# Group 0 of an attention + MoE kernel: triples of rows, transposes by half pairs between the scores, w1(0) between the value loads

## The chip, the cores and the metric

The kernel runs on one core of a Trainium2 chip. The metric is device time in microseconds (us) of one execution; the median of several runs counts. Profiles show single executions: TensorE (PE, with its weight loads as PEld), VectorE (DVE), ScalarE (ACT), GpSimd (POOL) and SyncE (SP), which only issues DMAs here.

## What is computed

Attention with two kinds of heads, and a mixture of experts on its result:

```
q, k, v: [4 batches, 8 heads, 768 tokens, 64] fp32
heads 0, 2, 6 ("retrieval"):     causal attention over all keys
heads 1, 3, 4, 5, 7 ("streaming"): causal, only the first 4 keys (sinks)
                                   and a window of 64 keys
a   = softmax(q k^T / 8, masked); attn = a v
x   = attn as [3072 tokens, 512]
out = sum over 4 experts e of  p_e * (relu(x @ w1_e) @ w2_e)
      w1_e: [512, 1024], w2_e: [1024, 512], p = domain_probs / their sum
```

## The kernel before

Attention is done in eight groups, a batch's half of 384 rows each. The order of the instructions on every engine is written out by hand: `attention(b, c)` is a generator that yields after every piece of work, and a plan runs it either alone or between pieces of MoE work. Group 0 runs alone, as nothing else has its inputs yet. Behind it comes the first MoE stage, `plain_steps`: three row tiles times expert 0, 1, 2, ..., each with w1(e) (matmul L1095) and w2(e) (L1116); group 1's attention is put between these matmuls. Up to some 55 us this stage needs weights that are still being loaded. Later MoE stages use sums of weights and other lines (L1229, L1258, L1409), and the change does not touch them.

**x in blocks.** x stands transposed in `xT`, four blocks of 128 rows. Block 0 holds heads 0 and 4, block 1 heads 1 and 5, block 2 heads 2 and 6, block 3 heads 3 and 7. The first MoE matmuls take four tiles of hidden columns together, with the blocks in the order 0, 2, 1 for each, and block 3 of all four at the end.

**Group 0, step by step.**

- *Rows of q and k.* `q32` and `k32` lie in `hA`, which the MoE uses only later. One DMA for each head loads its 384 rows as three blocks of 128 tokens (partition p, block j: token 128 j + p); a packet is one row of 64 fp32, 256 bytes. SyncE's queue issues k of all heads and q of heads 4 to 7, ScalarE's queue q of heads 0 to 3.
- *Transposes* (`transposes(hp)` for head pair hp): three fp32 `nc.tensor.transpose` for q and three for k (L576), each for 128 tokens and two heads, into one PSUM bank `ps`. VectorE or ScalarE then evict the bank as f16 to `qT` (L594), `kR` (retrieval keys, L602) or `kS` (streaming keys, L618), and the four sink keys beside them (L626).
- *Scores* (L693 for q and k, L705 for the mask, which is added by a matmul with the identity). ScalarE takes Exp (L711) into `es`.
- *Values* of a retrieval head (L756): 65 columns, of which the last is the sum. VectorE divides (L781 to L785), into `x_one` or `x_pair`, and `x_transposes` (L805, L809) bring them into `xT`. Values of a streaming head (L828) come out transposed, with the sums in the other half of the partitions: ScalarE takes Ln (L846) and Exp of minus that (L856, or L861 for two heads at once), and VectorE multiplies into `xT` (L851, "scaling").
- *Warm-up matmuls* (`warm_up`, L448): products of zeros, 8 at the start, 5 before scores 0, 8 before scores 2, and some of 256 columns before values of heads 3, 4, 5, 6, 7.
- *Masks*: `bC` (causal) and `bS` (streaming, three tiles of 160 columns) are made on GpSimd before its loads (L457 to L509).

**GpSimd's loads.** GpSimd's queue casts fp32 to f16 while it loads. Its order is: v of head 0, the masks, v of heads 2, 1, 3, 4, 6, 5, 7, w1(0) as two DMAs (the two halves of the partitions), w2(0), clears for group 1, w1(1). After that, one-element copies `landed(...)` (L521, "seen") make GpSimd wait until a load is there before it issues more: after w1(0) come k and q of heads 0 to 3 of group 1, after w2(0) comes w2(1), after these q the other heads, v and w1(2), and so on up to w2(2) and w1(3).

**Group 1** already loads "triples": `load_triples` gives partition p the tokens 3p, 3p + 1, 3p + 2, in a row in memory, for four heads at a time. Its transposes are f16 matmuls of half width (64 columns of lhsT, one head each, rhs the identity, L579), so that a bank holds the tokens in the order j, p; VectorE puts them in order while it evicts (L594, L602, L618 with rearranged views).

Of the kernel before, what the change touches and what calls it, by code (L numbers as in the profile page):

```python
# [11 lines left out]
FP32 = mybir.dt.float32  # L12
# [7 lines left out]
def kernel(  # L20
# [33 lines left out]
    nc = tc.nc  # L54
# [259 lines left out]

    def sink_row(h):

        t = v_tiles(0, 0, h)
        nc.vector.tensor_copy(
            out=t[0:NS, :, own_v(h)],
            in_=v_s32[:, h : h + 1, :].to_broadcast([NS, TC, D]),  # L320
        )
# [9 lines left out]

    def load_w1(e, f0, f1):
        x = moe_w1[e].rearrange("(u c d) f -> u d c f", u=2, c=DMP)
        for u in range(2):
            gp.dma_start(
                out=w1sb[half(u), e * DMP : (e + 1) * DMP, f0:f1],
                in_=x[u, :, :, f0:f1],
            )
# [61 lines left out]
    def rows32(n):  # L400
        x = hA[:, n * 6 * H * D : (n + 1) * 6 * H * D].bitcast(FP32)
        return x.rearrange("p (j h d) -> p j h d", j=3, h=H)

    q32, k32 = rows32(0), rows32(1)
    v_s32 = early[0:NS, 0:1024].bitcast(FP32).rearrange("p (h d) -> p h d", h=H)
    for h in range(H):
        if h == 2:
            nc.sync.dma_start(
                out=v_s32, in_=v[0, :, 0:NS, :].rearrange("h r d -> r h d")
            )  # L410
        nc.sync.dma_start(out=k32[:, :, h, :], in_=rows_of(k, 0, h, 0))
        if h == HP:

            nc.scalar.add_instruction(
                mybir.InstLoadActFuncSet(
                    name=nc.get_next_instruction_name(),
                    engine=ENG.Activation,
                    act_func_set_id=[x.name for x in SETS].index(
                        "natural_log_exp_and_others"
                    ),  # L420
                )
            )
        eng = nc.scalar if h < HP else nc.sync
        eng.dma_start(out=q32[:, :, h, :], in_=rows_of(q, 0, h, 0))
    nc.sync.dma_start(
# [6 lines left out]
    )  # L432
    nc.vector.memset(warm.bitcast(FP32), 0.0)
    nc.vector.memset(eps, 1e-9)
    nc.vector.memset(ones, ONES)
# [3 lines left out]
    zero(nc.vector, kR[0][:, 0, :, :, :])  # L439
    zero(nc.vector, kS[:, 0, :, :, :])  # L440
    nc.vector.tensor_copy(out=ident16, in_=ident32)
# [12 lines left out]

    def mask_c(x, keep, drop):

        gp.memset(x, keep)  # L457
        for i in range(2):
            gp.affine_select(
                out=x[:, i * P : (i + 1) * P], in_=x[:, i * P : (i + 1) * P],  # L460
                compare_op=ALU.is_ge, fill=drop, base=0, pattern=[[1, P]],
                channel_multiplier=-1,
            )

    def mask_s(x, n, keep, drop):

        gp.memset(x, keep)
        gp.affine_select(
            out=x, in_=x, compare_op=ALU.is_ge, fill=drop,
            base=R0, pattern=[[0, n], [1, TQ]], channel_multiplier=-1,  # L470
        )
        gp.affine_select(
            out=x, in_=x, compare_op=ALU.is_ge, fill=drop,
            base=NW - 1 - R0, pattern=[[0, n], [-1, TQ]], channel_multiplier=1,
        )
        gp.memset(x[0:R0, :, :], drop)
        gp.memset(x[0:NS, :, 0:TK], keep)
        gp.affine_select(
            out=x[0:NS, 0, 0:TK], in_=x[0:NS, 0, 0:TK], compare_op=ALU.is_ge,
            fill=drop, base=-NW, pattern=[[1, TK]], channel_multiplier=-1,  # L480
        )
# [24 lines left out]

    mask_c(bC, 0.0, -60000.0)
    mask_s(bS[:, 0:2, :], 2, 0.0, -60000.0)
    gp.tensor_copy(out=bS[:, 2, :], in_=bS[:, 1, :])  # L509
    load_v(0, 0, [2, 1, 3, 4, 6, 5, 7])  # L510
    load_w1(0, 0, F)
    load_w2(0)
# [45 lines left out]
    def attention(b, c):  # L558
# [8 lines left out]
        def transposed(x, hp):  # L567

            if first or hp > 1:
                ps = bank()  # L570
            else:
                ps = pV.tile([P, 512], FP32, name="pV", bufs=2)
            for j in range(3):
                o = ps[:, j * P : (j + 1) * P]
                if first:
                    nc.tensor.transpose(o, x[:, j, 2 * hp : 2 * hp + 2, :], ident32)  # L576
                    continue
                for u in range(2):
                    nc.tensor.matmul(  # L579
                        out=o[u * D : (u + 1) * D, :],  # L580
                        lhsT=x[:, 2 * hp + u, j, :],
                        rhs=ident16,
                        start=True,
                        stop=True,
                    )
            return ps

        def transposes(hp):
            both_at_once = [] if first else [transposed(x, hp) for x in (qt16, k16)]
            for x, is_k in ((q32 if first else qt16, 0), (k32 if first else k16, 1)):  # L590
                ps = transposed(x, hp) if first else both_at_once[is_k]
                if not is_k:
                    op = nc.scalar.copy if first and hp < 2 else nc.vector.tensor_copy
                    op(out=rows_in_order(qTs[b, c][:, hp, :]), in_=cols(ps))  # L594
                    if first:
                        yield t_ns
                    continue
                for u in range(2):
                    h = 2 * hp + u
                    r = slice(u * D, (u + 1) * D)  # L600
                    if RETR[h]:
                        nc.vector.tensor_copy(  # L602
                            out=rows_in_order(
                                kR[i][r, c, RH.index(h), :, :].rearrange(
                                    "r t x -> r (t x)"
                                )
                            ),
                            in_=cols(ps[r, :]),
                        )
                        continue  # L610
                    n = SH.index(h)
                    x_in, x_out = ps[r, 0:CH], kS[r, c, :, n, R0:P]
                    if first:
                        x_in = x_in.rearrange("r (t x) -> r t x", x=TK)
                    else:
                        x_in = x_in.rearrange("r (j t p) -> r j t p", j=3, t=TC)
                        x_out = x_out.rearrange("r t (p j) -> r j t p", j=3)
                    nc.vector.tensor_copy(out=x_out, in_=x_in)  # L618
# [6 lines left out]
                    src = src.rearrange("r (o x) -> r o x", o=1)  # L625
                    op(out=sinks, in_=src.to_broadcast([D, TC, NS]))  # L626
                yield 2 * t_ns if first else 3 * t_ns

        def rows_in_order(x):

            return x if first else x.rearrange("r (p j) -> r j p", j=3)

        def cols(x):
            x = x[:, 0:CH]
            return x if first else x.rearrange("r (j p) -> r j p", j=3)


        def score_tiles(h):
# [39 lines left out]
            ]  # L678

        es_of = {}  # L680
        pv_of = {}
        rc_of = {}
        scale_of = {}
        def scores(h):
            hp = h // 2
            es_of[h] = []
            for cols, parts, masks in score_tiles(h):
                ps = bank()
                if first and not es_of[h]:
                    warm_up(ps, {0: 5, 2: 8}.get(h, 0), P)  # L690
                ns = 0
# [119 lines left out]
        def values(h):  # L811
# [29 lines left out]
            r, o = half(u), half(1 - u)  # L841
            pair = first and h in (3, 4)
            if not pair or u == 0:
                rc_of[0] = att.tile([P, CH], FP32, name="rc", bufs=2)
            rc = rc_of[0]
            nc.scalar.activation(  # L846
# [11 lines left out]
            elif u == 0:  # L858
                scale_of[0] = scale
            else:  # L860
                nc.scalar.activation(out=rc, in_=rc, func=AF.Exp, scale=-1.0)  # L861
                later(scale_of[0], g)
                later(scale, g)
# [16 lines left out]
        if first:  # L880
            yield from transposes(0)
            yield from scores(0)
            sink_row(1)
            sink_row(3)
            yield from transposes(1)
            yield from scores(2)
            sink_row(4)
            sink_row(5)
            sink_row(7)
            yield from both(scores(1), values(0))  # L890
            yield from transposes(2)
            yield from both(scores(3), values(2))
            x_transposes(0)
            yield from scores(4)
            yield from transposes(3)
            yield from values(1)
            yield from both(scores(5), values(3))
            yield from both(scores(6), values(4))
            yield from both(scores(7), values(6))
            yield from values(5)  # L900
            at_once = behind.pop()
            v_steps = values(7)
            yield next(v_steps)
            x_transposes(6)
            at_once[1]()
            yield from v_steps
            tick(LAG)
# [760 lines left out]
```

## Time and profile before

| | |
|---|---|
| median of 3 runs | 376.3 us (376.27 to 376.65) |
| the profiled execution | 377.82 us |
| its span in the trace | 376.10 us |
| clock granted to TensorE | 1.00 |
| first MoE matmul starts | 21.50 us |
| TensorE busy | 367.1 us, 98% of the span |
| VectorE, ScalarE, GpSimd busy | 281.6, 227.3, 112.9 us |
| HBM, mean over the span | 136 GB/s |

Times in the profile count from the start of the span. A line such as "33.75 0.36 PE L579 MATMUL ... x6 [0.16 <-DMA q]" says: from 33.75 us, for 0.36 us, six matmuls of line 579 on TensorE, which before them stood idle for 0.16 until a DMA into q had landed. Matmuls are pipelined and their ends modelled, so the distance between starts tells more than the durations. In the table by stretches, each engine has its busy time and its instructions, then the clock granted to TensorE, the share of the DMA engines and GB/s. In the list of the chain each piece has its start, its length and what it was.

### The profile page before, as it was taken

Reading aid. Unit: us, or ns where it says so; the run is one execution under the profiler, and the core shown is the slowest. Engines: PE = TensorE matmul, PEld = TensorE weight load, DVE = VectorE, ACT = ScalarE, POOL = GpSimd, SP = SyncE. Lnnn points to the kernel's source line nnn. Section 1 sums busy time; section 2 is a strip of 40 time slices with the busy share of each in tenths; the row PEclk is TensorE's granted clock in tenths of the full one; section 3 lists DMA queues with packets and bytes.
Section 4 is the critical chain, followed back from the end, with each engine's and each line's share of the span. In section 5 each row is a group of like instructions: output and inputs, shape, how many; then the busy total and the mean of one; then the engine's idle time right before and its main releaser. Section 6 shows DMA issues by size and latency. Waiting matters only on the chain.

```text
span 376.1 us, 10310 instructions
## 1 busy us (share of the span) xinstructions
PE 367.1 (98%) x4221; PEld 312.4 (83%) x4221; DVE 281.6 (75%) x589; ACT 227.3 (60%) x475; POOL 112.9 (30%) x155
## 2 busy tenths in 40 slices
PE   8889999999999999999999999999999999999996
PEld 4755556568998999999989899988899998998996
DVE  7774768697788569868657858957767968989882
ACT  3863478557785785765676955774678362450630
POOL 8923664793058038115601650320000000000000
DMA  8999999999599579988904991971220200300101
GB/s 157 159 208 207 179 186 194 180 201 121 90 104 164 97 83 133 153 111 63 205 12 61 169 156 16 131 129 12 68 72 2 92 24 2 114 2 0 58 3 58
DMA packets 123748, 39.25 MB, mean 104 GB/s; under 512 B 113728, under 2 KB 116356, under 8 KB 123700
## 3 DMA queue, kind: packets, MB, share of 16 engines
q0 software_dynamic: 85824, 19.01, 58.6%
q1 hardware_dynamic: 36276, 19.18, 23.3%
q8 instruction: 33, 0.54, 0.7%
q10 hardware_dynamic: 1600, 0.39, 0.5%
q14 instruction: 15, 0.12, 0.1%
HBM read 44.89 MB, written 6.34 MB: 136 GB/s over the span
## 4 chain that ended last, share of the span: by engine, by line
PE 78%; DMA 12%; DVE 5%; POOL 3%; issue 1%; ACT 0%; DVEq 0%; POOLq 0%
PE pO L1409 29%; PE pA L1229 20%; PE pO L1258 9%; PE pO L1116 5%; DMA q<-in_q_dram 5%; PE pA L693 4%; DMA w2sb<-in_moe_w_dram 4%; PE pA L1095 3%; DMA w1sb<-in_moe_w_dram 2%; PE pV L1258 2%; PE pA L1258 2%; DVE xs L1180 2%; PE pV L828 2%; PE pV L756 2%; DMA xT<-x_pair 1%
## 5 line engine op out<-in xcount | busy, mean ns | idle before, releaser
L1409 PEld LDWEIGHTS <-hA 128*128 128x128 f16 x1104 | 104.9, 98 | 11.9
L1229 PE MATMUL pA<-xs,w1sb 128*128 128x256 f16 x768 | 97.1, 272 | 0.0
L1229 PEld LDWEIGHTS <-w1sb 128*128 128x128 f16 x768 | 71.7, 98 | 7.3
L1409 PE MATMUL pO<-w2sb,hA 128*128 128x256 f16 x640 | 76.8, 272 | 0.0
L711 ACT ACTIVATE es<-pA 128x384 f16<-128x384 f32 (+2 forms) x122 | 59.2, 512 | 26.4 <-PE pA L693 23.2
L1238 ACT ACTIVATE hA<-pA 128x512 f16<-128x512 f32 x96 | 57.2, 597 | 29.6 <-PE pA L1229 27.3
L306 POOL DMA_DIRECT2D vS<-in_v_dram x30 | 29.6, 986 | 113.7 <-PE pV L828 110.5
L1409 PE MATMUL pO<-tsb,hA 128*128 128x256 f16 x464 | 56.8, 272 | 0.0
L1180 DVE TENSOR_TENSOR xs<-xT,pB 128x1024 f16<-128x1024 f16 (+1 forms) x49 | 47.0, 977 | 3.7 <-DMA xT<-x_pair 3.7
L1014 DVE TENSOR_TENSOR hA<-hA 128x1024 f16<-128x1024 f16 x60 | 39.4, 684 | 0.6 <-PE pO L1409 0.3
L1108 ACT ACTIVATE hA<-pA 128x384 f16<-128x384 f32 (+1 forms) x64 | 22.2, 385 | 20.3 <-PE pA L1095 20.2
L1258 PEld LDWEIGHTS <-w1sb 128*128 128x128 f16 x512 | 31.3, 98 | 2.1 <-DVE xs L1014 0.8
L1095 PE MATMUL pA<-xT,w1sb 128*128 128x384 f16 (+1 forms) x256 | 30.4, 272 | 2.0 <-DMA w1sb<-in_moe_w_dram 1.9
L1116 PE MATMUL pO<-w2sb,hA 128*128 128x512 f16 x128 | 30.6, 379 | 0.1
L1095 PEld LDWEIGHTS <-w1sb 128*128 128x128 f16 x256 | 19.5, 98 | 11.0 <-issue 2.6
L1429 ACT COPY s<-pO 128x256 f32<-128x256 f32 x31 | 11.5, 372 | 27.3 <-PE pO L1409 21.8
L851 DVE TENSOR_TENSOR xT<-pV,rc 64x384 f16<-64x384 f32 x37 | 20.5, 554 | 9.3 <-ACT rc L856 6.8
L722 DVE TENSOR_TENSOR es<-es,mS 128x384 f16<-128x384 f16 (+1 forms) x40 | 13.8, 344 | 18.0 <-ACT es L711 17.9
L846 ACT ACTIVATE rc<-pV,eps 64x384 f32<-64x384 f32 x37 | 21.3, 575 | 7.0 <-PE pV L828 6.4
L1275 DVE CUSTOM_DVE_ANT_0 hA<-pO,s 128x512 f16<-128x512 f32 x26 | 17.7, 688 | 9.9 <-PE pO L1258 8.5
L1268 ACT COPY s<-pO 128x512 f32<-128x512 f32 x39 | 22.7, 588 | 3.2 <-PE pO L1258 3.0
L693 PE MATMUL pA<-qT,kR 128*128 128x128 f16 (+2 forms) x141 | 23.1, 261 | 0.4 <-DVE kR L602 0.4
(170 smaller groups left out, 527.6 us busy)
## 6 DMA issues: line engine op xcount, KB each, us to landing
pB<-p_rows SPq DMA_DIRECT2D x10, 512.0 KB
out_dram<-o SPq DMA_DIRECT2D x19, 256.0 KB
w1sb<-in_moe_w_dram POOLq DMA_DIRECT2D x8, 512.0 KB, 9.2
w2sb<-in_moe_w_dram POOLq DMA_DIRECT2D x4, 1024.0 KB, 13.3
vS<-in_v_dram POOLq DMA_DIRECT2D x30, 112.0 KB, 4.8
k_rows<-in_k_dram POOLq DMA_DIRECT2D x18, 128.0 KB, 5.1
q<-in_q_dram POOLq DMA_DIRECT2D x18, 128.0 KB, 6.4
vR<-in_v_dram POOLq DMA_DIRECT2D x24, 48.0 KB, 5.5
```

The source lines that it names most:

```text
L306: gp.dma_start(out=t[:, :, own_v(h)], in_=windows_of(v, b, h, c))
L693: nc.tensor.matmul(out=ps[:, o : o + nq], lhsT=key_tile(b, c, h, t), rhs=qTs[b, c][:, hp, q0 : q0 + nq], start=(n == 0 or not first), stop ...
L711: nc.scalar.activation(out=es[:, 0:cols], in_=ps[:, 0:cols], func=AF.Exp, scale=SC)
L1014: nc.vector.tensor_tensor(out=out, in0=a, in1=b, op=ALU.subtract)
L1095: nc.tensor.matmul(out=pss[ft][:, 0:cols_n], lhsT=w1_tile(e, ct, ft), rhs=x[:, ct, :], start=(n == 0), stop=(n == DMP - 1),)
L1116: nc.tensor.matmul(out=ps_o, lhsT=hs[:, ft, j * P : (j + 1) * P], rhs=w2sb[:, e * FTP + ft, :], start=(ft == 0), stop=(ft == FTP - 1),)
L1180: nc.vector.tensor_tensor(out=o, in0=xin, in1=pb.to_broadcast([P, DMP, n, P]), op=ALU.mult)
L1229: nc.tensor.matmul(out=ps[:, f * PC : (f + 1) * PC], lhsT=w1_tile(e, ct, f0 + f), rhs=xs[:, ct, :], start=(ct == 0), stop=(ct == DMP - 1),)
L1238: nc.scalar.activation(out=blocks[:, b0 : b0 + 2, k0 : k0 + 2, :].rearrange("p t f x -> p f t x"), in_=ps.rearrange("p (f t x) -> p f t x" ...
L1258: nc.tensor.matmul(out=ps[:, f * P : (f + 1) * P], lhsT=w_tile(e, w[:, ct, :], f), rhs=a[:, ct, :], start=(first and f == 0 and ct == 0), ...
L1268: nc.scalar.copy(out=kept[n], in_=ps)
L1409: nc.tensor.matmul(out=ps, lhsT=a[:, k, :], rhs=b(k), start=(first and k == 0), stop=(k == KT - 1), skip_group_check=not first,)
```

## The change

1. *Triples of rows for group 0.* q and k of heads 2 to 7 are loaded two heads at a time, partition p with the tokens 3p, 3p + 1, 3p + 2 (768 bytes in a row): six DMAs instead of twelve. Heads 0 and 1 stay as they were.
2. *Transposes by half pairs.* For these heads a block of q or k is transposed by six fp32 matmuls, each of one head's 64 columns with the fp32 identity, instead of three `transpose`. They write the bank with a stride of three columns, in the natural order of the tokens. Group 1's f16 halves do the same, and all evictions read the bank straight. In group 0 these blocks use the two banks of pool `pO`.
3. *Order.* Before, both halves of a pair (q and k) were transposed together. Now the blocks stand one by one between the scores: q of heads 2, 3; scores 0; k of 2, 3; scores 1; q of 4, 5; scores 2; k of 4, 5; scores 3 and values 0; q of 6, 7; scores 4; k of 6, 7; scores 5 and values 2; values 1; scores 6 and values 4; values 3; scores 7 and values 6; values 5; x transposes of head 6; values 7. Three warm-up matmuls stand before scores 0, none before scores 2.
4. *Sinks.* Five copies of sink rows of v become three larger ones, earlier. The copies of sink keys of heads 1 and 3 are put off to a set place.
5. *Masks.* One memset on VectorE clears both masks; the streaming mask is cut out of one tile of 160 columns and then copied, the last copy on VectorE. `kS` is cleared in four pieces.
6. *Loads.* v of 2, 1, 3; first half of w1(0); v of 4, 6; second half; v of 5, 7; w2(0).
7. *Exp for two heads at once* for heads 1 with 4 and 3 with 5, instead of 3 with 4.

The diff, cut:

```diff
-    for h in range(H):
+    for h in range(0, H, 2):
...
-        nc.sync.dma_start(out=k32[:, :, h, :], in_=rows_of(k, 0, h, 0))
+        pair_of_triples(nc.sync, k, k32, h)
...
+    def pair_of_triples(eng, x, dst, h):
+        if h == 0:
+            for u in range(2):
+                eng.dma_start(out=dst[0][:, :, u, :], in_=rows_of(x, 0, u, 0))
+            return
+        eng.dma_start(
+            out=dst[1][:, h - 2 : h, :, :].rearrange("p h j d -> p h (j d)"),
+            in_=x[0, h : h + 2, 0:CH, :].rearrange("h (p j) d -> p h (j d)", j=3),
+        )
...
+    nc.vector.memset(early[:, 1536:2272].bitcast(FP32), 0.0)
...
-    zero(nc.vector, kS[:, 0, :, :, :])
+    for t in range(TC):
+        zero(nc.vector, kS[:, 0, t : t + 1, :, :])
...
-    mask_s(bS[:, 0:2, :], 2, 0.0, -60000.0)
-    gp.tensor_copy(out=bS[:, 2, :], in_=bS[:, 1, :])
-    load_v(0, 0, [2, 1, 3, 4, 6, 5, 7])
-    load_w1(0, 0, F)
+    mask_s(bS, 0.0, -60000.0)
+    nc.vector.tensor_copy(out=bS[:, 2, :], in_=bS[:, 1, :])
+    load_v(0, 0, [2, 1, 3])
+    load_w1(0, 0, F, 0)
+    load_v(0, 0, [4, 6])
+    load_w1(0, 0, F, 1)
+    load_v(0, 0, [5, 7])
     load_w2(0)
...
-            if first or hp > 1:
+            if first and hp:
+                ps = pO.tile([P, 512], FP32, name="pO", bufs=2)
+            elif first or hp > 1:
                 ps = bank()
...
+            natural = ps[:, 0:CH].rearrange("r (x j) -> r j x", j=3)
             for j in range(3):
-                o = ps[:, j * P : (j + 1) * P]
-                if first:
-                    nc.tensor.transpose(o, x[:, j, 2 * hp : 2 * hp + 2, :], ident32)
+                o = natural[:, j, :]
+                if first and hp == 0:
+                    nc.tensor.transpose(
+                        ps[:, j * P : (j + 1) * P], x[0][:, j, :, :], ident32
+                    )
                     continue
                 for u in range(2):
                     nc.tensor.matmul(
                         out=o[u * D : (u + 1) * D, :],
-                        lhsT=x[:, 2 * hp + u, j, :],
-                        rhs=ident16,
+                        lhsT=x[1][:, 2 * hp - 2 + u, j, :] if first else x[:, 2 * hp + u, j, :],
+                        rhs=ident32 if first else ident16,
...
-                    warm_up(ps, {0: 5, 2: 8}.get(h, 0), P)
+                    warm_up(ps, {0: 3}.get(h, 0), P)
...
-            pair = first and h in (3, 4)
+            pair = first and {1: 1, 4: 1, 3: 3, 5: 3}.get(h)
...
             yield from transposes(0)
+            yield from transposes(1, 0)
+            put_off.pop(0)()
+            sink_row(1, 2)
             yield from scores(0)
-            sink_row(1)
-            sink_row(3)
-            yield from transposes(1)
+            yield from transposes(1, 1)
+            sink_row(4, 2)
+            sink_row(7)
+            yield from scores(1)
+            put_off.pop(0)()
+            yield from transposes(2, 0)
             yield from scores(2)
...
+            yield from values(1)
+            yield from both(scores(6), values(4))
             x_transposes(0)
-            yield from scores(4)
-            yield from transposes(3)
-            yield from values(1)
-            yield from both(scores(5), values(3))
-            yield from both(scores(6), values(4))
+            yield from values(3)
             yield from both(scores(7), values(6))
             yield from values(5)
-            at_once = behind.pop()
-            v_steps = values(7)
-            yield next(v_steps)
             x_transposes(6)
-            at_once[1]()
-            yield from v_steps
+            yield from values(7)
```

## The prediction, made before the changed kernel ran

> **What bounds the kernel now.** I read the page first (busy shares and the chain that ended last), then TensorE's waits, then the timeline of the first 55 us, because the diff touches only group 0 and what is loaded beside it.
>
> ```profile
> span 376.1 us, 10310 instructions
> PE 367.1 (98%) x4221; PEld 312.4 (83%) x4221; DVE 281.6 (75%) x589; ACT 227.3 (60%) x475; POOL 112.9 (30%) x155
> PE 78%; DMA 12%; DVE 5%; POOL 3%; issue 1%; ACT 0%; DVEq 0%; POOLq 0%
> ```
>
> TensorE is busy 98% of the span, so what is not TensorE work is small. The chain holds 12% of transfers, and its list in time order shows where:
>
> ```profile
> 12.53 8.84 DMA w1sb<-in_moe_w_dram
> 22.40 11.30 DMA q<-in_q_dram
> ...
> 41.02 13.57 DMA w2sb<-in_moe_w_dram
> 54.63 1.02 PE pO L1116 x4
> ```
>
> Up to 54.6 us the chain is GpSimd's load stream: w1(0), then q of group 1, then w2(2). From there it is TensorE alone. TensorE's waits after 20 us say what that stream costs:
>
> ```profile
> PE pA L1095 <- DMA w1sb<-in_moe_w_dram: 1.9, 2, 1.1
> PE pV L579 <- DMA q<-in_q_dram: 0.2, 1, 0.2
> ```
>
> TensorE's timeline, with the waits in brackets:
>
> ```profile
> 4.73 1.51 PE L576 MATMUL pA<-early,hA 128*128 128x128 f32 x6
> 7.38 0.89 PE L576 MATMUL pA<-early,hA 128*128 128x128 f32 x6
> 18.36 0.24 PE L756 MATMUL pV<-vR,es 128*128 128x65 f16 x2 [1.02 <-ACT es L711]
> 21.50 5.61 PE L1095 MATMUL pA<-xT,w1sb 128*128 128x384 f16 x32 [1.11 <-DMA w1sb<-in_moe_w_dram]
> 33.75 0.36 PE L579 MATMUL pV<-ident,q 128*64 128x128 f16 x6 [0.16 <-DMA q<-in_q_dram]
> 33.94 0.33 PE L579 MATMUL pV<-ident,k 128*64 128x128 f16 x6
> 47.85 0.32 PE L1095 MATMUL pA<-xT,w1sb 128*128 128x384 f16 x1 [0.80 <-DMA w1sb<-in_moe_w_dram]
> ```
>
> So three stretches: group 0 up to 21.5, ended by w1(0) (1.11); then up to 54.6 three stalls on loads: 0.16, 0.80, and about 0.25 between the seven matmuls that begin at 54.15 (pitch about 0.03) and 54.63, which the chain gives to w2(2). Together 1.2. Then 321 us that the change does not touch.
>
> But behind the 1.11 stands group 0 itself, almost as late (ScalarE's timeline, VectorE's, and the table by stretches):
>
> ```profile
> 19.54 0.57 ACT L846 ACTIVATE rc<-pO,eps 64x384 f32<-64x384 f32 x1 [0.30 <-PE pO L828]
> ```
> ```profile
> 21.02 0.56 DVE L851 TENSOR_TENSOR xT<-pO,rc 64x384 f16<-64x384 f32 x1
> ```
> ```profile
> 6.00:20.40 14.40, 12.82 (x141) 10.39 (x138) 11.08 (x31) 10.56 (x27) 12.48 (x22) 1.00 1.21 167
> ```
>
> The first MoE matmuls take x blocks 0, 2, 1: the third needs heads 1 and 5, and head 5's scaling ends at 21.02 + 0.56 = 21.58. The third matmul starts at about 21.83. An earlier w1(0) alone would gain 0.25. The last line is the table by stretches: TensorE 12.82 busy in the 14.40 from 6.0 to 20.4.
>
> **The loads.** GpSimd's rows between the masks and w1(0):
>
> ```profile
> 4.25 1.46 POOL L472 TENSOR_SCALAR_AFFINE_SELECT early<-early 128x320 f16<-128x320 f16 x1
> 6.98 0.78 POOL L304 DMA_DIRECT2D vR<-in_v_dram  x1
> 11.92 1.24 POOL L335 DMA_DIRECT2D w1sb<-in_moe_w_dram  x2
> 21.42 0.18 POOL L521 COPY seen<-w1sb 1x1 f16<-1x1 f16 x1 [2.75 <-DMA w1sb<-in_moe_w_dram]
> ```
>
> The masks run from 2.40 to 6.98 = 4.58. Two memsets (0.33, 0.36) go to VectorE, the two selects over 320 columns (0.46, 1.46) become 160 wide, the memsets on 320 shrink, one copy stays: by halves 0.54 + 0.3 + 0.6 + 0.3 + 0.25 + 0.3 + 0.3 = 2.6. The v loads thus begin 2 us earlier, at about 5.0. VectorE's new memset of 368 fp32 columns, by its 1.12 for 1280, costs 0.32 at about 1.5 us; the mask's last copy (0.31 on GpSimd) is also VectorE's now. Cover: both lie before the first keys arrive in PSUM (VectorE waits 0.77 until 6.28); without it 0.6 on the head's start.
> The first half of w1(0) is issued after three v loads instead of seven, the second after five; two v loads (1.4 of issue) move behind it. They serve heads 5 and 7, the last values, so if they land by 15 us nobody waits.
> On SyncE, twelve issues of q and k, 0.53 apart (0.82 to 8.31), become about seven, done by about 5; ScalarE's queue issues three instead of four. A packet grows from 256 to 768 bytes. The slices of 1 us show 7 to 15 us at 154 168 158 183 141 109 69 141 GB/s, against some 205 later: 8 x 205 - 1123 = 517 KB too little, 2.5 us of transfer. w1(0) therefore lands 2 to 3.5 us earlier, at 18 to 19.4, and what is queued behind it follows, held by the "seen" copies in the same order. The stalls need 0.16, 0.80 and 0.25: all three go, **-1.15** (I leave the 0.05 that a changed tile costs). The 1.11 goes too, but then head 5's scaling is next.
>
> **The transposes.** Heads 0 and 1 stay as they are. For heads 2 to 7, 18 fp32 transposes go: six take 0.89, of which the last one's length is about 0.25, so 0.109 apart: 18 x 0.109 = 1.96. In come 18 pairs of half matmuls, fp32, 64 columns wide, written to PSUM with a stride of three. No row has that form. The nearest in form are the f16 halves (33.75 to 33.94: six in 0.19, a pair 0.063): there two halves run side by side, since a whole f16 matmul of 128 columns takes 0.055. The nearest in type is the transpose, 0.109. Ends: 0.109, if the halves run side by side at the transpose's rate; 0.218, if one after the other. I take the middle, **0.16**, as each end shares form or type with one row. The pairs: 18 x 0.16 = 2.88. Six changes of tile size there and back: 34.21 - 33.94 = 0.27 against 0.19 gives 0.08 each way, 6 x 0.17 = 1.0.
> The row of the transposes is one thing, rules of the Trainium skill speak against reading it so. "TensorEngine Tiling (Array Packing)", section Restrictions, says that column tiling rules out the transpose mode for FP32 input, and "FP8 and Floating Point Precision", section TensorE Precision Notes, that true FP32 takes four passes. By these a half would be an ordinary fp32 product, as an estimate 4 x 0.055 = 0.22 for a pair side by side, and the total about nil; one after the other 0.44 and some +4. No row of this trace shows an fp32 product that is not a transpose.
> Ten small warm-up matmuls go: five took 0.107 each (half the rate; six transposes at 4.73 show 0.25 each too), eight 0.055; 0.97 less three of 0.107 is -0.65. The change to full rate comes between 6.0 and 7.4 after unbroken work; the halves now fill that place, so 0; if it came one block later, +0.5.
> Net TensorE work: 2.88 + 1.0 - 1.96 - 0.65 = **+1.3**.
>
> **The end of group 0.** Until head 5's last value matmul (result at 19.50) TensorE did about 11.9 of the 12.82, as values 7 and the last x transposes lie behind both before and after. Idle time in the stretch was 1.58, of it 1.02 at 18.36, where ScalarE's Ln and Exp stood ahead of an Exp of scores. ScalarE has the same work (10.56 of 14.40), and 1.3 more on TensorE gives it time, so most of that closes. New are a wait for the triples of heads 2 and 3 at 6.0 (they are there by 7.38 already before) and one for the bank that head 1's scaling holds when values 6 begin; behind that one stand the values of 5 and 7. I take 0.6 for all waits, between 0.3 and 1.6 (all of the old ones).
> Values 5 then end at 6.0 + 11.9 + 1.3 + 0.6 = 19.8. Behind them Ln 0.57, Exp 0.52 for heads 3 and 5 at once, two scalings of 0.56: 2.2. Third MoE matmul at 22.0 instead of 21.83: **+0.2**.
>
> **The rest.** Sink rows: five copies (0.60 for two, 0.83 for three) become three larger ones, on VectorE with 11.08 of 14.40 busy; half a microsecond later keys at worst. Group 1's f16 halves are also written with the stride of three, and VectorE reads them straight: 0.55 instead of 0.80 each. TensorE does not wait there; nil. If the strided write cost TensorE as much as the strided read costs VectorE (0.80/0.55 = 1.45), eight blocks of 0.19 would add 0.7.
>
> **Sum:** +0.2 - 1.15 = **-0.95**. The profiled execution took 377.82 (376.10 and 1.72 around it), 1.5 over the median of the runs, 376.3; the change in stretch is the same in either: 375.4, or 376.9 for the profiled one.
>
> **Rivals.** A measurement of this kernel tells about 0.2% (0.75 us) from no change.
> *Same:* the pair costs 0.2 to 0.23, one half after the other. Each 0.05 a pair is 18 x 0.05 = 0.9, so 0.218 gives -0.95 + 1.04 = +0.1: 376.4. For it: no fp32 row runs side by side. Against: the f16 halves do. 0.20.
> *Slower:* one mechanism, the half pairs: one after the other and held by the strided write, 0.218 x 1.45 = 0.32, is 18 x 0.16 = 2.9 more, +1.9: 378.2. It decides from 0.16 + 0.95/18 = 0.21 a pair. Its far end is a pair of halves at the price of two slow transposes (0.21 apart at 4.73): 0.43, +3.9. For it: TensorE is the bound in every stretch, so nothing hides its work. Against: nothing in the rows needs that price. 0.30.
> *Loads not earlier:* GpSimd's issue is then not what holds w1(0), and the stalls stay: -0.95 + 1.15 = +0.2, 376.5. For it: after 15 us the transfers already run at 193 to 220 GB/s. Against: the hole of 517 KB before. 0.10.
> *The forecast* (pairs of 0.11 to 0.18): 0.40, with 374.4 to 376.0 its own range; at 0.109 the sum is -1.9.
>
> **Chances.** Faster: 0.36 of the forecast, 0.06 of the same case and 0.01 of the late loads = 0.43. Same: 0.04 + 0.11 + 0.05 = 0.20. Slower: 0.30 + 0.03 + 0.04 = 0.37. The range goes from 374.2 (pairs side by side) to 379.0 (a pair of 0.36), as the signs are mixed.
>
> **What would show it.** Right: the six halves of a block in about 0.5; "seen" of w1(0) at 18 to 19.4; the first MoE matmuls waiting for VectorE's xT and not for w1sb; no waits for w1sb, q or w2sb between 22 and 55. Wrong: blocks of 0.7 or more; ScalarE's wait still 1 us at values 6; w1sb still named after 21 us; transposes of heads 2 and 3 waiting a microsecond for their triples.

## The result, and the profile after

The changed kernel takes 379.1 us (median of 4 runs, 379.01 to 379.35) beside 376.4 for the kernel before in the same comparison: ratio 1.0072, 95% interval 1.0054 to 1.0089, that is **2.0 to 3.4 us slower**. The forecast was 1 us faster, the range ended at 379.0.

The page of the changed kernel, its span, busy times and chain:

```profile
span 377.3 us, 10389 instructions
PE 368.9 (98%) x4265; PEld 313.5 (83%) x4265; DVE 279.4 (74%) x592; ACT 227.2 (60%) x474; POOL 110.6 (29%) x153
PE 95%; DVE 2%; DMA 1%; ACT 1%; issue 0%; ACTq 0%
```

The 12% of transfers in the chain are down to 1%, as forecast; TensorE took their place, at no gain. Its timeline (line 604 is the half matmul, 465 a warm-up, 1112 the MoE's first matmul). "The third MoE matmul" in what follows is the first that needs heads 1 and 5, and its start marks the end of group 0:

```profile
6.54 0.88 PE L604 MATMUL pO<-early,hA 128*64 128x128 f32 x12 [1.14 <-DMA hA<-in_q_dram]
7.35 0.34 PE L465 MATMUL pA<-early 128*128 128x128 f16 x3
...
19.13 0.81 PE L465 MATMUL pV<-early 128*128 128x256 f16 x6 [0.98 <-DVE xT L868]
...
23.41 5.29 PE L1112 MATMUL pA<-xT,w1sb 128*128 128x384 f16 x30 [1.11 <-DVE xT L868]
...
35.10 0.52 PE L604 MATMUL pV<-ident,q 128*64 128x128 f16 x6
35.41 0.54 PE L604 MATMUL pV<-ident,k 128*64 128x128 f16 x6
35.88 3.42 PE L1112 MATMUL pA<-xT,w1sb 128*128 128x384 f16 x20
```

Three things are to be seen. A block of six halves is twelve records and occupies TensorE for 7.35 - 6.54 = 0.81. The MoE's first matmuls no longer wait for w1; the third starts at 23.41 and waits for VectorE's xT. And group 1's f16 halves take 0.31 and 0.47 to the next start, where they took 0.19 and 0.27. GpSimd's row shows that w1(0) was there long before:

```profile
18.13 0.18 POOL L541 COPY seen<-w1sb 1x1 f16<-1x1 f16 x1 [1.65 <-DMA w1sb<-in_moe_w_dram]
```

The transfers, in slices of 1 us from 0, run at over 330 GB/s from 5 to 8 us, where before they ran at 154 to 233:

```profile
GB/s 0 5 210 209 177 337 331 330 179 157 189 187 168 210 201 191 149 197 215 209 217 205 217 207 215 208 191 201 202 208 215 211 236 193 193 175 157 171 186 203
```

### The profile page after: what moved, and what is told of

It is laid out like the page before. It is cut to its first block, busy times and chain, and to the rows that moved or that the text cites. A ratio compares the mean times of both kernels' runs of the same rounds, so it can differ in the third digit from the quotient of the medians.

```text
span 377.3 us, 10389 instructions
## 1 busy us (share of the span) xinstructions
PE 368.9 (98%) x4265; PEld 313.5 (83%) x4265; DVE 279.4 (74%) x592; ACT 227.2 (60%) x474; POOL 110.6 (29%) x153
## 4 chain that ended last, share of the span: by engine, by line
PE 95%; DVE 2%; DMA 1%; ACT 1%; issue 0%; ACTq 0%
PE pO L1426 31%; PE pA L1246 22%; PE pO L1275 9%; PE pA L1112 7%; PE pO L1133 7%; PE pA L710 6%; PE pV L1275 2%; PE pV L773 2%; PE pA L1275 2%; PE pV L845 2%; PE pO L604 1%; DMA hA<-in_q_dram 1%; DVE xs L1197 1%; DVE xT L868 1%; PE pA L1518 0%; PE pA L604 0%
## 6 DMA issues: line engine op xcount, KB each, us to landing
w2sb<-in_moe_w_dram POOLq DMA_DIRECT2D x4, 1024.0 KB, 12.1
```

## The experiments

Times are medians beside those of the kernel before on the same chip (376.3 to 376.4); intervals are those of the ratio, times 376.3.

### Was the first profile of before a usual execution?

**e1**, the kernel before once more, unedited.

> The kernel before once more, for a second profile. Its first profiled execution had a span of 376.1 us and 377.82 in all, 1.4 over the median of its timed runs, 376.4; those of the changed kernel had spans of 377.3 to 377.6, with its profiled one among them. If the first profile was an unusual execution, this one has a span near 374.7, and one of the three load stalls (0.16 at 33.75, 0.80 at 47.85, about 0.25 at 54.6) or the 1.11 before the first MoE matmul is shorter or gone. If timed and profiled executions differ by themselves in this kernel, it has 376 again with the same stalls.

Span 374.1, time 375.76. TensorE's waits after 22 us, and the MoE's start:

```profile
PE pA L1095 <- DVE qT L594: 0.3, 1, 0.3
PE pO L1258 <- ACT hA L1308: 0.2, 1, 0.2
PE pV L756 <- ACT es L711: 0.2, 1, 0.2
```
```profile
20.70 0.48 PE L1095 MATMUL pA<-xT,w1sb 128*128 128x384 f16 x2 [0.51 <-DMA w1sb<-in_moe_w_dram]
21.44 5.29 PE L1095 MATMUL pA<-xT,w1sb 128*128 128x384 f16 x30 [0.25 <-DVE xT L851]
```

No load stall is left after 22 us; the wait for w1 is 0.51 instead of 1.11. Of 22 timed executions of before in one comparison 13 have spans of 374.2 to 374.6, eight 374.8 to 376.8, one 473.5; so this profile lies at the lower end of the usual ones, and the first, with 376.1, outside them. The first profile is 0.4 behind e1 at the third MoE matmul and 1.4 behind at 62 us; the rest of the 2.0 between the spans comes later, with a wait of 0.5 at L1258 that e1 lacks. A median execution is 0.5 longer than e1 and may hold a part of the stalls; no profile shows one. Most of what the earlier loads were to win is not there to be won in most executions. Further comparisons use this second profile: third MoE matmul at 21.44 before, 23.41 after, **+1.97**.

### The half pairs

**e6**, the kernel before with group 0's transposes as ordinary matmuls:

```diff
-                    nc.tensor.transpose(o, x[:, j, 2 * hp : 2 * hp + 2, :], ident32)
+                    nc.tensor.matmul(
+                        out=o, lhsT=x[:, j, 2 * hp : 2 * hp + 2, :], rhs=ident32,
+                        start=True, stop=True,
+                    )
```

> The kernel before with group 0's 24 fp32 transposes made as ordinary matmuls of full width with the fp32 identity, nothing else. In the changed kernel the two halves of a pair start 7 ns apart and each makes two passes 0.109 apart, so a pair takes 0.218. Theory that the two passes come from leaving the transpose, not from the half width: each of the 24 takes 0.218 here as well, two records each, 24 x 0.109 = 2.6 more on TensorE. About 1 us of it may hide in the waits of before (1.0 for es at values 6, 0.5 for w1), so 377.9 to 379. Rival, that the width of 64 makes the second pass: a full product takes 0.109, and the time stays 376.3.

378.87, +2.0 to +3.8. The answers for the line of the transposes, first in e1, then in e6:

```profile
L576 PE MATMUL pA<-early,hA x24: 272/273/448, 4.7 to 13.0; 128*128 128x128 f32 x24
```
```profile
L576 PE MATMUL pA<-early,hA x48: 275/275/450, 4.7 to 15.4; 128*128 128x128 f32 x48
```

24 instructions leave 24 records as transposes and 48 as products, of the same length. So the second pass comes from leaving the transpose, at full width as well. Of the 2.6 worked out, 2.4 arrive at the third MoE matmul (23.85, in e1 21.44), and the time rose by about as much: little of it hid.

```profile
23.85 5.29 PE L1098 MATMUL pA<-xT,w1sb 128*128 128x384 f16 x30 [0.27 <-DVE xT L854]
```

**e3**, the changed kernel with all halves written side by side, evictions in order:

```diff
-                o = natural[:, j, :]
+                o = ps[:, j * P : (j + 1) * P]
```

> As e2_group1_straight, and in group 0 too the fp32 half matmuls write their bank side by side; the evictions put the tokens in order. In the changed kernel such a block of six halves takes 0.81 (twelve records 0.067 apart, two for each matmul). Theory that the stride costs here what it costs the f16 halves (0.052 instead of 0.032 apart): blocks fall to about 0.5, six times 0.3 = 1.8 less work on TensorE, time about 376.5. Rival, that an fp32 product of half width costs this much whatever it writes: blocks stay at 0.8, and time stays at that of e2_group1_straight or up to 0.5 above it, as evictions of 0.55 become 0.80.

387.62, +9.5 to +12.1. The block is unchanged (next start at 7.55):

```profile
6.74 0.88 PE L614 MATMUL pO<-early,hA 128*64 128x128 f32 x12 [1.24 <-DMA hA<-in_q_dram]
7.55 0.34 PE L465 MATMUL pA<-early 128*128 128x128 f16 x3
```

The stride costs the fp32 halves nothing; the rival holds there. That the time is 8.5 us above the changed kernel's was expected by neither. TensorE's waits hold 6.6 of it: three times the scores stand until VectorE has evicted the streaming keys (`kS`) of the next pair.

```profile
10.90 0.24 PE L726 MATMUL pA<-qT,kS 128*128 128x160 f16 x1 [1.53 <-DVE kS L655]
17.38 0.24 PE L726 MATMUL pA<-qT,kS 128*128 128x160 f16 x1 [3.50 <-DVE kS L655]
23.60 0.24 PE L726 MATMUL pA<-qT,kS 128*128 128x160 f16 x1 [1.54 <-DVE kS L655]
```

The changed kernel has none of these waits: its scores 1 begin at 8.92 and run through, while the keys of head 3 are evicted at 9.62. So the edit brought more than slower evictions; that their writes into `kS` in steps of three make other heads' scores wait is likely and was not tested. The longest wait has a second part: two copies of sink rows took 3.85 together, the second alone 3.47.

```profile
10.87 3.85 DVE L320 CAST vS<-early 4x512 f16<-4x512 f32 x2
```

The evictions for which scores 3 wait are queued behind that copy. The half block after this wait takes 1.54 instead of 0.88 for its twelve records; the clock granted to TensorE from 6 to 20 us was 0.92. In the changed kernel the same two copies, at 10.21, take 1.07.

### The strided write

**e2**, the changed kernel with group 1's halves side by side (`o = natural[:, j, :] if first else ps[:, j * P : (j + 1) * P]`, and the old evictions for group 1).

> The changed kernel with group 1's f16 half blocks written side by side again, as before, and put in order by the evictions. Theory: the strided write itself slows TensorE. In the changed kernel's trace the q block takes 0.31 to the next start instead of 0.19, the k block 0.46 instead of 0.26, over four pairs of blocks 4 x 0.32 = 1.3 us. So they go back to 0.19 and 0.26, and the time falls by 1.2 to 1.3, to 377.8. Rival: the blocks got slower because of what else changed around them (loads that now run beside them, other evictions), and the order of the writes has no part in it: blocks stay at 0.31, time 379.1 or, with the slower evictions, 379.3.

```profile
35.54 0.36 PE L614 MATMUL pV<-ident,q 128*64 128x128 f16 x6
35.73 0.33 PE L614 MATMUL pV<-ident,k 128*64 128x128 f16 x6
36.00 3.42 PE L1128 MATMUL pA<-xT,w1sb 128*128 128x384 f16 x20
```

0.19 and 0.27 again: the order of the writes is what slows the f16 halves. The time is 378.52 (ratio 1.0082, 1.005 to 1.0113), which cannot be told from the changed kernel's 1.0072. In its profile the third MoE matmul came at 23.85 instead of 23.41, as the triples were waited for until 6.99 instead of 6.54, and the wait of 0.28 for qT was back. From the third MoE matmul to the scores at about 55 us it is 0.8 shorter.

**e5**, the other way round: the kernel before with group 1's writes strided and straight evictions.

> The kernel before with one thing of the change: group 1's f16 half blocks write their bank with a stride of three and the evictions read it straight. Theory that the strided write slows TensorE: q block 0.31 to the next start instead of 0.19, k block 0.46 instead of 0.26, over four pairs 1.27 more; the wait of 0.28 for qT behind the last pair (in the second profile of before) goes, as that eviction takes 0.55 instead of 0.80: +1.0, 377.3. Rival (the prediction's nil: the writes cost nothing and faster evictions gain): 376.0 to 376.3.

376.77: -0.1 to +0.9, less than the 1.0 expected. Its blocks take 0.31 for q, the wait for qT is gone, and its span is 0.7 longer than e1's. Over the same stretch it is 1.0 longer than e1. So the strided write is a loss on TensorE that the profiles show, of 0.8 to 1.0 us by 55 us, which the timing can't tell from nothing.

### The loads

**e7**, the kernel before with the change's masks and its order of v and w1(0); **e8**, with the masks alone.

```diff
-    load_v(0, 0, [2, 1, 3, 4, 6, 5, 7])
-    load_w1(0, 0, F)
+    load_v(0, 0, [2, 1, 3])
+    load_w1(0, 0, F, 0)
+    load_v(0, 0, [4, 6])
+    load_w1(0, 0, F, 1)
+    load_v(0, 0, [5, 7])
```

> The kernel before with the change's masks and order of v and w1(0) alone; q and k come by rows, head by head, in the old order of work. Theory from e4_rows_whole, where q of heads 6 and 7 landed only at 16.4: w1's halves, issued at 7 and 9 us, take the transfer rate from the rows, so the transposes of heads 6 and 7 wait to about 16 instead of starting at 12.5, and the time is 3 us or more over before, 379.5 to 381. Rival, that the row loads of e4 were late because of the order of SyncE's queue there (k of two heads, then q): no such wait here, w1 is there at 19 instead of 20.6, and the time falls by 0.5, to 375.8.

> As e7_before_masks_and_loads but w1(0) behind all v loads, as before: only the masks are shorter, and all of GpSimd's loads are issued 2 us earlier (v from 4.8, w1 from about 9.8). Theory that the early w1 is what starves the rows: fewer rows are still on their way at 9.8 than at 7, so the wait at heads 6 and 7 is shorter than in e7 but there, 0.5 to 2 us: 376.3 to 378. Rival: the rows are done by then, w1(0) is no longer waited for (0.5 and 0.25 in the second profile of before), 375.6.

e7: 378.44, +1.6 to +3.8. e8: 376.10, ratio 0.9994 (0.9975 to 1.0014), no difference. In both the v loads start at 5.86, not at 4.79 as in the changed kernel: one select on GpSimd takes 1.34 instead of 0.26 while VectorE clears `kS` in one piece. e7's waits of TensorE up to 22 us, its w1, and the w1 of e8:

```profile
PE pO L832 <- DMA vS<-in_v_dram: 1.2, 2, 0.9
PE pA L580 <- ACT es L715: 1.1, 1, 1.1
```
```profile
20.71 0.18 POOL L525 COPY seen<-w1sb 1x1 f16<-1x1 f16 x1 [3.14 <-DMA w1sb<-in_moe_w_dram]
```
```profile
20.23 0.18 POOL L522 COPY seen<-w1sb 1x1 f16<-1x1 f16 x1 [2.64 <-DMA w1sb<-in_moe_w_dram]
```

Its halves issued 3.8 and 2.4 us earlier than in e1, w1(0) is seen at 20.71, in e1 at 20.62 and in e8 at 20.23: here the place between the v loads gains nothing, and the values wait for v instead. The wait for q that the theory named did not show; the loss did, from another load. Only with the triples did w1 come at 18.1 or before.

**e4**, the changed kernel without triples and half pairs, group 1 written side by side, early w1 kept (the edit in outline):

```diff
-        pair_of_triples(...)             # two heads in one DMA
+        for u in range(2):
+            eng.dma_start(out=dst[:, :, h + u, :], in_=rows_of(x, 0, h + u, 0))
...
-    six half matmuls
+    nc.tensor.transpose(ps[:, j * P : (j + 1) * P], x[:, j, 2 * hp : 2 * hp + 2, :], ident32)
```

> The changed kernel without the triples and the half pairs: q and k of group 0 come by rows, head by head, as before, and each block is three fp32 transposes of full width; group 1 writes side by side. Order between the scores, sinks, masks, order of the loads, pairs of Exp as changed. Theory that the half pairs are what the change loses: blocks of 0.33 instead of 0.81 without a change of tile, 6 x 0.48 = 2.9 less on TensorE, of which the wait for rows at the start and the wait for head 1's bank (0.98) take some back; with the 1.2 of group 1, 379.1 - 1.2 - 2 = 375.9 or below, that is faster than before by what the earlier loads bring. Rival, that the new order loses it (waits of 1.14, 0.98 and 1.11 in the changed kernel's trace stay or grow when TensorE has less to do): 377.5 or more.

382.94, +5.7 to +7.4: in the range of the rival, by a wait that neither named:

```profile
16.38 0.87 PE L601 MATMUL pO<-early,hA 128*128 128x128 f32 x3 [5.38 <-DMA hA<-in_q_dram]
```

q of heads 6 and 7 came 5.4 us late. **e9** is e4 with w1(0) behind all v:

> As e4_rows_whole (rows of q and k head by head, fp32 transposes of full width, group 1 side by side), but w1(0) behind all v loads. What is left of the change is the order of the work, the sinks, fewer warm-ups, the other pairs of Exp and the shorter masks. In e4 the block of q of heads 6 and 7 waited 5.4 us for its rows. Theory: that wait came from w1's halves being issued at 7 and 9 us, so here it is gone or under 1 us, TensorE has 2.9 less to do in group 0 than in the changed kernel, and the time is 375.5 to 377, at or a little below before: the order itself costs nothing. Rival: the order costs by itself (1.0 at the start for rows of heads 2 and 3, 1.0 for head 1's bank, 1.1 before the third MoE matmul): 378 or more.

377.15, +0.2 to +1.7. The longest wait for rows is 1.0, so the 5.4 came from the early w1, which itself is seen only 0.2 earlier (19.14, in e9 19.35). The rest of e9 is the next question. **e10**, the changed kernel with w1(0) behind all v, was to show whether the early w1 is used:

> The changed kernel with w1(0) behind all v loads. In it w1(0) was seen at 18.1, while the third MoE matmul waited for head 5's scaling until 23.4: the early w1 is not used. Theory: w1(0) now lands at about 20, still before TensorE asks for it at 21.7, and the time stays at 379.1 within 0.4. Rival: w1's place matters in this kernel, for what it delays (group 1's loads are issued behind it, and stalls come back at 35, 49 or 56 us): 380 or more; or for what it was in the way of (v of 5 and 7): 378.5 or less.

Five executions took 378.72 to 382.93, +2.6 to +5.7, and the profiled one 988 us. In that one TensorE ran at less than half its usual speed (1.87 for a block of six halves), so its times explain nothing; but GpSimd's loads ran as in the others, and w1(0), issued behind all v, is seen as early as in the changed kernel:

```profile
18.07 0.18 POOL L538 COPY seen<-w1sb 1x1 f16<-1x1 f16 x1 [1.23 <-DMA w1sb<-in_moe_w_dram]
```

So in none of three pairs (e7 and e8, e4 and e9, the changed kernel and e10) does the place between the v loads bring w1(0) more than 0.2 earlier, and profiles with the loads of e9 differ by more than that among themselves (18.94 in e13, 20.14 in e12). What the time of e10 holds besides stays open.

### The order

e9's waits up to 24 us (line 457 is a warm-up, 598 a transpose, 1118 the MoE):

```profile
PE pO L598 <- DMA hA<-in_q_dram: 1.6, 2, 1.0
PE pO L457 <- DVE early L440: 1.3, 1, 1.3
PE pA L1118 <- DVE xT L874: 1.1, 1, 1.1
PE pV L457 <- DVE xT L874: 1.0, 1, 1.0
PE pO L598 <- DVE rs L804: 0.9, 1, 0.9
```

With the old transposes TensorE has 2.9 less to do, and yet its third MoE matmul starts at 22.30: 0.86 behind e1 and only 1.11 ahead of the changed kernel. The rest became waiting: for rows, 0.9 put down to VectorE, and the same 1.0 for head 1's bank and 1.1 for head 5's scaling.

**e13** is e9 with `pair = first and {3: 3, 5: 3}.get(h)`: heads 1 and 4 take Exp singly. **e14** has `{}`: none paired.

> As e9_new_order_alone, but heads 1 and 4 take Exp each by itself, as head 1 did before; 3 and 5 stay paired. Theory that the bank held for head 1's scaling is what the order costs: head 1 is scaled at about 16.7 instead of 18.0, the wait of 0.98 at values 6 goes, values 5 end about 0.9 earlier and the time is that of before, 376.3 to 376.6. Rival that a wait takes its place: ScalarE has 0.52 more and the scores of head 6 get their second Exp that much later, at 17.8 to 18.2, where values 6 now begin at 18.7: a wait for es instead of the bank, gain 0.2 to 0.5, time 376.7 to 377.0.

> As e13_order_head1_alone, and heads 3 and 5 by themselves too. In e9 head 5's scaling stands behind head 3's on VectorE, both behind one Exp (Ln at 19.96, scaled at about 22.2, 2.3 us). Theory: with head 3 scaled earlier the tail is 0.57 + 0.52 + 0.56 and the third MoE matmul starts 0.4 to 0.6 earlier than in e13, at the price of 0.52 on ScalarE before the last Exp of scores 7, which only values 7 need: 0.2 to 0.5 below e13, 376.0 to 376.5. Rival: the Exp of 3 ahead of the scores of 7 delays values 7 and its block is needed by the 13th MoE matmul, or the tail does not matter: same as e13 or slower.

e13: 376.84 (+0.2 to +1.5); e14: 377.74 (+1.1 to +2.3). e13's profile:

```profile
PE pO L598 <- DVE kS L657: 1.2, 1, 1.2
PE pO L598 <- DMA hA<-in_q_dram: 1.0, 2, 0.5
PE pA L1118 <- DVE xT L874: 0.9, 1, 0.9
PE pV L779 <- ACT es L734: 0.6, 1, 0.6
```

The wait for the bank went and one of 0.6 for es came; the third MoE matmul moved from 22.30 to 21.68, but 0.37 of that stood already at the q block of heads 6 and 7 (12.09, in e9 12.46), where the edit had not yet acted. The 0.3 in the time is within the noise. e14 was slower: the tail shrank (0.27 before the third matmul), but the last x transposes waited 1.3 for head 6's division on VectorE. Of its 1.0 behind e13 at the third matmul (22.70), 0.7 stood already at that q block, after 1.3 of waiting for rows.

**e15**, the same edit as e13 in the changed kernel:

> The changed kernel with heads 1 and 4 taking Exp each by itself. In it values 6 waited 0.98 for head 1's bank until 19.13. Theory: the wait shrinks to that for es (0.2 to 0.5 left), and the time falls by 0.4 to 0.8, to 378.3 to 378.7. Rival that the half blocks set the pace and the wait is only slack: 379.1.

381.94, against both. Again one copy of sink rows (head 7's) took 4.05 of this:

```profile
10.47 4.39 DVE L320 CAST vS<-early 4x512 f16<-4x512 f32 x2
```

TensorE waited 2.7 for an eviction behind it. The edit acts only after that point, so its effect was not measured. Moving these copies ahead of scores 0, here and in e13, would have tested it; there is no result of such a run.

**e11** and **e12** put scores 0 ahead of the q block of heads 2 and 3, in the changed kernel and in e9:

```diff
-            yield from transposes(1, 0)
             put_off.pop(0)()
             sink_row(1, 2)
             yield from scores(0)
+            yield from transposes(1, 0)
```

> The changed kernel with scores 0 before the q block of heads 2 and 3, as before the change. The q block waited 1.14 for its triples (from 5.4 to 6.54), with scores 0 queued behind it. Theory that this wait is on the path: TensorE does scores 0 in it (0.6 of work, which itself waits for VectorE's key copy to about 6.5), and the time falls by 0.3 to 0.8. Rival: what ends group 0 is the later chain of the values, which has slack before it in ScalarE and VectorE: same within 0.2, 379.0.

> As e9_new_order_alone with scores 0 before the q block of heads 2 and 3. Where e9 has a wait of about 1 us for rows at the start, this has less: 0.3 to 0.8 below e9. If e9 is near before, this is the version that may beat both kernels, at 375.3 to 376. Rival: the end of group 0 is set by Ln, Exp and scalings of the last heads, so nothing changes against e9.

e11: 378.78, 0.3 below the changed kernel, with a third MoE matmul at 23.41 to the hundredth as there. That looks as if the wait of 1.14 for triples were slack, but the profile, of the longest of six executions, doesn't show it. The wait for triples is gone, and the start was late instead: the first transposes began at 5.33, in the changed kernel at 4.56.

```profile
5.33 0.89 PE L599 MATMUL pA<-early,hA 128*128 128x128 f32 x6 [0.47 <-DMA hA<-in_q_dram]
```

And in e2 triples that came 0.45 later put the third MoE matmul 0.44 later. So the wait is on the path as far as the profiles show. e12: 377.57, not better than e9; its profile has 1.7 of waiting for rows in one wait.

**e16**, the kernel before with `warm_up(ps, {0: 3}.get(h, 0), P)`:

> The kernel before with the change's warm-ups alone: three before scores 0 instead of five, none before scores 2 instead of eight. Theory of the prediction: pure TensorE time, 2 x 0.06 to 0.1 and 8 x 0.055, so 0.55 less before 9 us; but in before TensorE then waits for rows, for es (1.0 at values 6) and for w1(0), so most of it turns into waiting: 376.0 to 376.4. Rival that they keep TensorE's clock up: transposes of heads 2 and 3 twice as long (0.9 more), 376.8 or more.

376.45, 0.0 to +0.6: no gain from ten matmuls less, and the transposes of heads 2 and 3 keep their 0.89. A wait of 0.72 for qT stands before scores 2, where the eight were.

No version beat the kernel before; e5, e8 and e16 can't be told from it.

## Why the prediction was wrong, point by point

- **The stalls, -1.15: the step that failed first.** They are in the trace I used and not in e1, where TensorE waits for no load after 22 us. The text noted that the profiled execution was 1.5 over the median and then carried its stalls to the median unchanged. They were a large part of what made that execution long: between the third MoE matmul and 62 us it falls 1.0 behind e1.
- **Half pairs.** Taken 0.16, between 0.109 and 0.218; the records give 0.218: two halves start 7 ns apart, so they do run side by side, and each makes two passes 0.109 apart. With the change of tile a block is 0.81, six are 4.85 instead of the 3.88 of the sum, +1.0. My upper end had the right number for a wrong reason (halves one after the other): luck. That true FP32 takes four passes ("FP8 and Floating Point Precision", section TensorE Precision Notes, in the Trainium skill) gave, as an estimate, 0.22 for a pair: the trace agrees in the time, with two records of 0.109 and not four of 0.055. I weighed that rule and took a lower value. (The lower end of the range, 374.2, is 0.2 below what the text's own -1.9 gives; nothing hangs on it.)
- **The end of group 0.** Forecast +0.2 at the third MoE matmul, measured +1.97 against e1 (+1.58 against the first profile). By e9 against e1, 0.86 of it is the order with the old transposes, its waits for rows included; by e9 against the changed kernel, 1.11 is the half pairs together with their triples and the early w1, though the work of the half pairs is 2.9. How the 1.11 splits among the three was not measured. The values of head 5 ended at 21.0 instead of 19.8. I had put all waits together at 0.6; the trace has 1.14 for the triples and 0.98 for the bank. The bank wait that I named is 0.98 alone; it comes from pairing head 1's Exp with head 4's, and e13 shows a wait for es of 0.6 behind it. The tail from Ln of head 5 to its scaling was forecast 2.2 and is 2.3 (21.07 to about 23.4).
- **Strided f16 writes.** Taken as nil, bounded at 0.7. The blocks show 0.32 for each of the first three pairs and, with the wait for qT gone, 0.8 in all by 55 us (+2.74 there, after +1.97).
- **Warm-ups.** Taken as -0.65 of TensorE time. With the old order, leaving the ten out gained nothing (e16): a wait of 0.72 came where the eight had been. What they bring in the changed kernel was not measured.
- **Right:** w1(0) at 18 to 19.4 (18.1); the first MoE matmuls waiting for xT and not for w1; no stalls on loads from 22 to 55; masks 2 us shorter (v from 4.79). The early arrival of w1(0) is right in its time and not in all its reasons: the place between the v loads shows no part in it (e10).
- **The rival "slower"** named the half pairs, held by the strided write, one after the other, at 0.32. Half pairs are part of the loss, but at 0.218, which that text counted as no change; without the stalls, as in e1, the point from which they decide was far lower. The stride slowed the f16 halves, not these.

The sum by e1's profile: +1.97 in group 0, +0.8 in group 1's halves, 0 for stalls, together +2.7 by 64 us, where the median rose by 2.7. The two spans differ by 3.2, as e1 is shorter than a median execution; of the other 0.5, 0.2 lies between 64 us and the last matmuls (372.12, in e1 369.23), and 0.3 behind them. It was not followed.

## What to carry to other kernels

Before a stall in a profile is counted as a gain, hold the profiled execution against the timed ones: if it is longer by just about those stalls, a second profile is worth more than any sum. A change of layout that forces a transpose into an ordinary product pays for it in passes, and TensorE at 98% hid little of that (2.4 of 2.6 showed in e6). Moving a load ahead of others in its queue did not bring it earlier here and delayed what it passed (e4 against e9, e7 against e8); and an earlier load gains only until the next late thing, here a scaling 0.25 us behind.

## What the runs showed of the hardware

- An fp32 transpose of 128 columns is one record 0.109 after the last, an fp32 product by the identity two (e1, e6).
- A stride of three in PSUM slowed f16 halves from 0.19 to 0.31 for six, and left fp32 halves at 0.81 (e2, e3).
- The same copy of 4 x 256 on VectorE took 0.27 (e2), 0.73 (changed kernel), 3.47 (e3) and 4.05 us (e15), beginning at 10.6 to 11.2 us. In e2 GpSimd stood idle from 10.3 to 11.2, when the copy ran; in the others it issued loads or cleared tiles all the while. What holds the copy is not shown.
- After TensorE stood still for 5.4 us (e4) a block of three transposes took 0.66 to the next start instead of 0.36, and TensorE's granted clock from 6 to 20 us was 0.82 instead of 1.00 (e9).
